# Cluster attention and two wide layers on one core: GpSimd in written order, the steps of a pair spread anew over its ticks, values' high halves on GpSimd

## The chip, the core and the metric

One core of a Trainium2 chip: TensorE (PE, matmuls; PEld its weight loads), VectorE (DVE), ScalarE (ACT), GpSimd (POOL), and SyncE (SP), whose queue issues this kernel's DMA transfers. The metric is the device time of one execution in microseconds (us).

## The reference

```python
def _attn_ref(q, k, v, centroids):
    ...
    q_assign = np.argmax(np.einsum('bhsd,hcd->bhsc', q_n, c_n), axis=-1)
    k_assign = np.argmax(np.einsum('bhsd,hcd->bhsc', k_n, c_n), axis=-1)
    mask = q_assign[:, :, :, None] == k_assign[:, :, None, :]
    scores = scale * np.matmul(q, k.transpose(0, 1, 3, 2))
    scores = np.where(mask, scores, -1000000000.0)
    scores = scores - np.max(scores, axis=-1, keepdims=True)
    attn = np.exp(scores)
    attn = attn / (np.sum(attn, axis=-1, keepdims=True) + 1e-09)
    return np.matmul(attn, v).astype(np.float32)

def _moe_ref(x, w_in, w_out, alpha):
    h = x @ w_in
    g = np.maximum(h, 0.0) + alpha * np.minimum(h, 0.0)
    return (g @ w_out).astype(np.float32)

def _moe2_ref(x, w_in, w_out):
    h = x @ w_in
    g = np.maximum(h, 0.0) + np.log1p(np.exp(-np.abs(h)))
    return (g @ w_out).astype(np.float32)
```

`q`, `k` and `v` are 2 x 8 heads x 768 x 64, with 16 centroids a head; `q_n`, `k_n`, `c_n` are the rows over their norms. A query attends only to keys of its own cluster. The heads side by side are the 1536 x 512 input of `_moe_ref` (2048 hidden units), whose output is that of `_moe2_ref`.

## The kernel before

*Numbers.* Products keep float32's precision with two fast matmul operands: a value is split into a rounded high half and the low rest (`hi`/`lo`, `ph`/`pl`, `xh`/`xl`, `gh`/`gl`, `vv` with both), and the products of the halves are summed in PSUM.

*Attention.* Heads go in 8 pairs (a batch and two heads). A pair has 12 units, one for each block of 128 queries of each head, and a loop of 96 **ticks** (lines 777 to 805) is a software pipeline over the units. In tick u, in this order, TensorE makes the scores of unit u (L586, L587: `ak`, `aq` are keys and queries, `mk`, `mq` carry the mask as 16 extra rows), ScalarE copies out a finished output (`drain`, every second tick), takes the exponentials of unit u-1 (L601), VectorE the maximum of unit u (L592); then the steps registered for the tick's early phase run; TensorE transposes unit u-2 (L614), ScalarE and VectorE split it into `ph` (L630) and `pl` (L634); TensorE multiplies with the values, `attend` (L644), for unit u-4; last run the steps of the late phase.

*Steps of a pair.* What has to be ready before pair n's units is cut into named steps (`steps_of`), and a table gives each its tick: value x means tick 12(n-2) + x, late phase; a half (6.5) means the next whole tick, early phase. The pair's own units are at x = 24 to 35. So each tick holds steps of pair n+2 (x under 12) and of pair n+1 (x from 12). `STEADY` serves most pairs, `FIRST`, `SECOND` and `THIRD` the first three; `PRELUDE` lists what comes before tick 0. The steps: `sq0/1` square the tokens, `fold0` to `fold2` sum them by halving, `inv0` to `inv2` make the inverse norm `rinv` (`inv_norm`, L127 to L141); `hik/hiq`, `lok`, `lq0/1` split keys and queries; `dk/dq` the centroid products (L397), `de` copies them out, `dt` transposes them, `dn` (L436) scales by `rinv`, `mx`, `eq`, `m2` find the best centroid, `ot` transposes the one-hot rows, `mr` makes the mask rows (L495 on ScalarE, L497 on VectorE); `op` copies operands by DMA (L536), `mk` the masks (L542, L543); `va` splits the values (L556, L557); `go` makes the pair ready. Loads are `load_tok`, `load_dim` and `load_v`, each with one buffer. `finish(n)` normalises a pair's output: at ticks +7 to +16 after the pair, with `rp`, a transposed reciprocal made by TensorE (L717) and multiplied in by VectorE (L721) at +12 and +14. `dps`, `dt`, `ot` and `rp` all use the one PSUM buffer with tag "m" (`ps_m`, bufs=1).

*Order.* Inside `tc.manual_schedule` the named engines, PE, ACT and DVE, execute in the order written; GpSimd and SP are ordered by the framework's scheduler, which works on its own timing model. Waits are generated from the tiles that are read and written. The manual part ends with the last unit (L781); the layers are ordered by the scheduler on all engines.

*Layers.* 16 blocks of hidden units each; weights arrive as 64-bit floats, are turned to float32 by ScalarE, VectorE and GpSimd (`to_float32`) and split. `first` makes hidden products (L843), `activate` and `complete` the activation (L855 to L884), `second` the output products (L902) into four accumulators, `close` adds them up (L917) and sends them out.

## Time and profile before

| | us |
|---|---|
| median of 3 runs (816.08 to 821.30) | 818.02 |
| the profiled execution | 819.76 |
| its span, first to last instruction | 817.8 |
| busy in the span: PE / DVE / ACT / POOL | 784.9 / 599.4 / 490.6 / 345.0 |
| mean granted TensorE clock | 0.976 |

The profile is of one execution. A row of the view of stretches has the stretch, its length, then busy us and, in brackets, instructions of PE, PEld, DVE, ACT and POOL, the granted clock, the DMA share and GB/s. Busy time of PE counts matmuls to a modelled end, so overlapping ones make it look fuller than it is. A row of a timeline has start, duration, engine, line, operation, written tile <- read tiles, shape, count, and in brackets the idle time of the engine before it and what ended that.

### The profile page before, as it was taken

Reading aid. Unit: us, or ns where it says so; the run is one execution under the profiler, and the core shown is the slowest. Engines: PE = TensorE matmul, PEld = TensorE weight load, DVE = VectorE, ACT = ScalarE, POOL = GpSimd, SP = SyncE. Lnnn points to the kernel's source line nnn. Section 1 sums busy time; section 2 is a strip of 40 time slices with the busy share of each in tenths; the row PEclk is TensorE's granted clock in tenths of the full one; section 3 lists DMA queues with packets and bytes.
Section 4 is the critical chain, followed back from the end, with each engine's and each line's share of the span. In section 5 each row is a group of like instructions: output and inputs, shape, how many; then the busy total and the mean of one; then the engine's idle time right before and its main releaser. Section 6 shows DMA issues by size and latency. Waiting matters only on the chain.

```text
span 817.8 us, 11947 instructions
## 1 busy us (share of the span) xinstructions
PE 784.9 (96%) x4137; PEld 672.7 (82%) x4137; DVE 599.4 (73%) x953; ACT 490.6 (60%) x992; POOL 345.0 (42%) x355
## 2 busy tenths in 40 slices
PE   7799999989999978999999999999999999999997
PEld 5699988989998767888888888888888888888886
DVE  5799989989999979446835934979459568764443
ACT  5589988978899868535635634675366245343221
POOL 3765766657244565215404503766045036023000
PEclk9599999999999998999999999999999999999999
DMA  9976675664451244201401401322013012000102
GB/s 256 235 178 152 167 181 134 158 163 103 100 160 42 79 147 161 79 1 60 148 0 52 135 20 52 97 85 77 1 52 130 25 52 77 27 1 1 43 35 77
DMA packets 27195, 76.50 MB, mean 94 GB/s; under 512 B 4512, under 2 KB 7456, under 8 KB 27136
## 3 DMA queue, kind: packets, MB, share of 16 engines
q1 hardware_dynamic: 27136, 75.75, 32.6%
q8 instruction: 32, 0.52, 0.3%
q14 instruction: 27, 0.22, 0.1%
HBM read 49.36 MB, written 3.15 MB: 64 GB/s over the span
## 4 chain that ended last, share of the span: by engine, by line
PE 76%; DVE 11%; DMA 5%; POOL 3%; issue 2%; ACT 2%; SPq 0%; DVEq 0%; POOLq 0%; ACTq 0%
PE acc L902 29%; PE hp L843 27%; PE pt L614 6%; PE o L644 6%; PE s L587 3%; PE s L586 3%; DVE r L173 2%; DVE pl L634 2%; DMA tok<-in_qk_tok_dram 2%; DVE nm L592 1%; DMA mq<-hi 1%; POOL t L178 1%; DVE m L168 1%; DMA mq<-mrow 1%; PE dps L397 1%
## 5 line engine op out<-in xcount | busy, mean ns | idle before, releaser
L843 PE MATMUL hp<-xh,ih 128*128 128x512 f32 x384 | 149.8, 391 | 2.7 <-DVE gl L884 2.4
L843 PE MATMUL hp<-xl,ih 128*128 128x512 f32 x384 | 150.0, 391 | 0.0
L843 PE MATMUL hp<-xh,il 128*128 128x512 f32 x384 | 149.7, 390 | 0.0
L181 POOL TENSOR_TENSOR il<-t,ih 128x512 fp32r<-128x512 f32 x32 | 43.9, 1372 | 197.5 <-ACT ih L180 187.1
L884 DVE TENSOR_TENSOR gl<-hp,gh 128x512 fp32r<-128x512 f32 x96 | 65.9, 687 | 70.8 <-ACT gh L883 70.6
L883 ACT CAST gh<-hp 128x512 fp32r<-128x512 f32 x96 | 56.5, 588 | 88.9 <-PE acc L902 69.0
L592 DVE TENSOR_REDUCE nm<-s 128x1 f32<-128x768 f32 x96 | 91.0, 948 | 11.9 <-PE s L587 11.4
L634 DVE TENSOR_TENSOR pl<-pt,ph 128x384 fp32r<-128x384 f32 x192 | 97.4, 547 | 1.9 <-ACT ph L630 1.2
L178 POOL TENSOR_TENSOR t<-m,r 128x512 uint32<-128x512 uint32 x64 | 85.2, 1331 | 29.3 <-DVE r L173 16.4
L601 ACT ACTIVATE e<-s,nm 128x768 f32<-128x768 f32 x96 | 87.9, 916 | 8.1 <-DVE nm L592 8.1
L614 PE MATMUL pt<-ident,e 128*128 128x128 f32 x576 | 85.4, 282 | 6.8 <-DVE pl L634 6.8
L630 ACT CAST ph<-pt 128x384 fp32r<-128x384 f32 x192 | 83.7, 490 | 13.6 <-PE pt L614 12.5
L843 PEld LDWEIGHTS hp<-xh,ih 128*128 128x128 f32 x384 | 72.2, 188 | 18.2 <-DVE gl L884 2.9
L865 ACT ACTIVATE sp<-a 128x512 f32<-128x512 f32 x48 | 30.4, 633 | 92.4 <-DVE a L861 92.4
L843 PEld LDWEIGHTS hp<-xh,il 128*128 128x128 f32 x384 | 72.4, 189 | 15.2
L843 PEld LDWEIGHTS hp<-xl,ih 128*128 128x128 f32 x384 | 72.2, 188 | 14.9
L614 PEld LDWEIGHTS pt<-ident,e 128*128 128x128 f32 x576 | 68.9, 145 | 17.2 <-DVE pl L634 12.6
L902 PE MATMUL acc<-gh,oh 128*128 128x512 f32 x192 | 73.8, 396 | 4.4 <-ACT gh L883 4.4
L902 PE MATMUL acc<-gl,oh 128*128 128x512 f32 x192 | 75.9, 396 | 0.2 <-DVE gl L884 0.2
L902 PE MATMUL acc<-gh,ol 128*128 128x512 f32 x192 | 75.5, 393 | 0.0
L586 PE MATMUL s<-ak,aq 128*128 128x384 f32 x192 | 70.6, 367 | 4.7 <-DMA mk<-lo 4.7
L902 PE MATMUL acc<-oh,gh 128*128 128x512 f32 x192 | 74.7, 389 | 0.0
(168 smaller groups left out, 1679.9 us busy)
## 6 DMA issues: line engine op xcount, KB each, us to landing
raw<-in_w_in_dram SPq DMA_DIRECT2D x32, 512.0 KB, 3.3
raw<-in_w_out_dram SPq DMA_DIRECT2D x32, 512.0 KB, 3.3
tok<-in_qk_tok_dram SPq DMA_DIRECT2D x8, 768.0 KB, 5.4
ak<-hi SPq DMA_DIRECT2D x32, 192.0 KB, 3.0
dim<-in_qk_dim_dram SPq DMA_DIRECT2D x6, 768.0 KB, 6.9
rawv<-in_v_dram SPq DMA_DIRECT2D x8, 384.0 KB, 3.2
aq<-hi SPq DMA_DIRECT2D x16, 192.0 KB, 3.7
mk<-lo SPq DMA_DIRECT2D x16, 192.0 KB, 3.4
```

The lines of the kernel that those rows point to most:

```text
L178: nc.gpsimd.tensor_tensor(out=t.bitcast(U32), in0=mu, in1=r, op=ALU.add)
L586: nc.tensor.matmul(s[:, c, 0:HS], lhsT=aq[:, qs], rhs=ak[:, ks], start=True, stop=False)
L592: nc.vector.tensor_reduce(out=nm, in_=st[u]["s"][:, :, 0:HS], axis=AX.XY, op=ALU.max, negate=True)
L601: nc.scalar.activation(out=e.rearrange("p (a j) c -> p a (j c)", a=2), in_=st[u]["s"][:, :, 0:HS], func=AF.Exp, bias=st[u]["nm"], scale=1. ...
L614: nc.tensor.transpose(pt[:, j * P : (j + 1) * P], st[u]["e"][:, 3 * a + j, :], ident)
L630: nc.scalar.copy(out=dh, in_=src)
L634: nc.vector.tensor_tensor(out=dl, in0=src, in1=dh.bitcast(F32), op=ALU.subtract)
L644: nc.tensor.matmul(acc[key][:, 0:QG], lhsT=vv[:, j, 2 * hh : 2 * hh + 2, :].rearrange("p a d -> p (a d)"), rhs=grp[key][part][:, j, :], st ...
L843: nc.tensor.matmul(hp, lhsT=a_[:, cs], rhs=b_[:, c, ts], start=n == 0, stop=n == 3 * NC_ - 1)
L883: nc.scalar.copy(out=gh, in_=hp)
L884: nc.vector.tensor_tensor(out=gl, in0=hp, in1=gh.bitcast(F32), op=ALU.subtract)
L902: nc.tensor.matmul(accs[c], lhsT=a_, rhs=b_, start=opens and n == 0, stop=closes and n == 2)
```

## The change

GpSimd joins the engines of the manual part. The loads become steps of their own (`lt`, `ld`, `lv`, and "values" in the prelude) in place of calls within `sq1`, `lq1` and `va`; SP stays with the scheduler. The operand copies and the values' split are cut into smaller steps (`op0a` to `op1c`, `va0`, `va1`). The values' high halves are copied by GpSimd, mask rows are all made on ScalarE, and the norm's scaling runs on the engine of its neighbours (GpSimd for all pairs but the first). The sum of a drained output is written one tick later, with a third buffer for `tmp` and `rest`. All tables are new, pair 1's squares and folds leave the prelude, and the last pair has a table of its own. In the last three steps of the last layer TensorE follows the written order.

```diff
 STEADY = dict(
-    hik=-1, lok=3, sq0=0, hiq=2, sq1=2, fold0=3, fold1=4, fold2=6, lq0=5, dk0=4, dq0=6, de0=6.5,
-    inv0=7, lq1=8, inv1=9, dk1=9, dq1=10, inv2=10, de1=10.5, dt=11, dn=11, op0=11, mx=11.5, eq=15,
-    m2=16, va=18, ot0=19, mr0=19, op1=19, ot1=20.5, mr1=20.5, mk0=20.5, mk1=20.5, go=22,
+    sq0=0, sq1=1, lt=1.5, fold0=2, hik=3, lok=3, hiq=4, lq0=5, dk0=5, fold1=6, dq0=6, de0=6.5, lq1=6,
+    fold2=7, ld=7, inv0=8.5, dk1=9, inv1=9, dq1=10, inv2=10, de1=10.5, dt=11, dn=12, mx=13, op0a=13.5,
+    op0b=14.5, op0c=15.5, eq=15.5, m2=17, ot0=19, mr0=19.5, ot1=20, va0=20, mr1=20.5, mk0=20.5, op1a=21,
+    op1b=22, va1=22, op1c=23, lv=23.5, mk1=24, go=23,
 )
 FIRST = dict(
-    mr0=23.5, mr1=23.5, mk1=23.5, va=24,
+    va0=24, mr0=25, mr1=25, mk1=25, op1c=25, va1=28, lv=29,
 )
 SECOND = dict(
-    dl0=12, dl1=12, inv0=12, de0=12.5, de1=12.5, inv1=13, inv2=13, dt=13, dn=14, mx=14, op0=14,
-    eq=15.5, m2=16, va=18, ot0=19, mr0=19, op1=19, ot1=20.5, mr1=20.5, mk0=20.5, mk1=20.5, go=22,
+    sq0=12.5, sq1=13, fold0=13, dl0=12, dl1=12, de0=12.5, de1=12.5, dt=13, lt=13, fold1=14, op0a=14,
+    fold2=15, op0b=15, inv0=15.5, op0c=16, inv1=16, inv2=16.5, dn=17, mx=17, eq=17.5, m2=18, ot0=19.5,
+    mr0=19.5, ot1=20, mr1=20.5, mk0=20.5, op1a=21, op1b=22, op1c=23, go=23, mk1=24, va0=25, va1=27, lv=28,
 )
 THIRD = dict(
-    hik=3, lok=3, sq0=0, hiq=4, sq1=2, fold0=4, fold1=5, fold2=6, lq0=5, dk0=5, dq0=6, de0=6.5,
-    inv0=7, lq1=8, inv1=9, dk1=9, dq1=10, inv2=10, de1=10.5, dt=11, dn=11, op0=11, mx=11.5, eq=15,
-    m2=16, va=18, ot0=19, mr0=19, op1=19, ot1=20.5, mr1=20.5, mk0=20.5, mk1=20.5, go=22,
+    sq0=5, sq1=7, lt=7.5, hik=7, lok=8, hiq=8, fold0=9, lq0=9, dk0=9, fold1=10, dq0=10, lq1=10, ld=10.5,
+    de0=10.5, dk1=11, fold2=11, inv0=11.5, dq1=12, inv1=12, de1=12.5, inv2=12.5, dt=13, dn=13.5, mx=14,
+    op0a=14.5, op0b=15.5, op0c=16.5, eq=16, m2=17, ot0=19, mr0=19.5, ot1=20, va0=20, mr1=20.5, mk0=20.5,
+    op1a=21, op1b=22, va1=22, op1c=23, lv=23.5, mk1=24, go=23,
 )
+LAST = dict(STEADY, op1a=19, op1b=20, va1=21, op1c=21, mk1=22, go=22)
 PRELUDE = [
     "warm 18", "sq0 0", "centroids_high", "red0 0", "centroids_low", "hik 0", "sq1 0", "lok 0",
     "red1 0", "hiq 0", "lq0 0", "dk0 0", "dq0 0", "inv0 0", "lq1 0", "inv1 0", "de0 0", "dk1 0",
-    "dq1 0", "inv2 0", "op0 0", "de1 0", "dt 0", "hik 1", "lok 1", "hiq 1", "warm 10", "dh0 1",
-    "dh1 1", "op1 0", "warm 10", "minus_alpha", "dn 0", "mx 0", "eq 0", "m2 0", "sq0 1", "sq1 1",
-    "fold0 1", "fold1 1", "fold2 1", "ot0 0", "lq0 1", "ot1 0", "rq0 0", "rk0 0", "rk1 0", "rq1 0",
-    "lq1 1", "go 0",
+    "dq1 0", "inv2 0", "op0a 0", "op0b 0", "op0c 0", "lt 0", "values", "de1 0", "dt 0", "hik 1", "lok 1",
+    "hiq 1", "warm 10", "dh0 1", "dh1 1", "op1a 0", "op1b 0", "warm 10", "minus_alpha", "dn 0", "mx 0",
+    "eq 0", "m2 0", "ot0 0", "lq0 1", "ot1 0", "rq0 0", "rk0 0", "rk1 0", "rq1 0", "lq1 1", "ld 1", "go 0",
...
-        nc.vector.tensor_scalar(out=s1, in0=s1, scalar1=0.5, scalar2=1e-6, op0=ALU.mult, op1=ALU.add)
+        eng.tensor_scalar(out=s1, in0=s1, scalar1=0.5, scalar2=1e-6, op0=ALU.mult, op1=ALU.add)
...
-            tc.manual_schedule(engines={mybir.EngineType.PE, mybir.EngineType.Activation, mybir.EngineType.DVE})
+            tc.manual_schedule(
+                engines={mybir.EngineType.PE, mybir.EngineType.Activation, mybir.EngineType.DVE, mybir.EngineType.Pool}
+            )
...
-        load_v(0)
...
-                if t == 1:
-                    load_tok(n + 1)
...
-                if t == 1 and n > 0:
-                    load_dim(n + 1)
...
-            def rows(t, eng):
+            def rows(t):
...
-                if eng is nc.scalar:
-                    nc.scalar.activation(out=q["mrow"][:, t, :], in_=src, func=AF.Identity, scale=mscale, bias=bias)
-                else:
-                    nc.vector.tensor_scalar(
-                        out=q["mrow"][:, t, :], in0=src, scalar1=mscale, scalar2=bias, op0=ALU.mult, op1=ALU.add
-                    )
+                nc.scalar.activation(out=q["mrow"][:, t, :], in_=src, func=AF.Identity, scale=mscale, bias=bias)
...
-            def operands(hh):
+            def operands(hh, part):
...
+                if part == 0:
+                    aq = ap3.tile([P, S], F32R, tag="aq", name="aq")
+                    ak = ap3.tile([P, S], F32R, tag="ak", name="ak")
+                    mq = ap3.tile([D + C, S], F32R, tag="mq", name="mq")
+                    mk = ap3.tile([D + C, S], F32R, tag="mk", name="mk")
+                    res.append((aq, ak, mq, mk))
+                aq, ak, mq, mk = res[hh]
...
-                ):
+                )[2 * part : 2 * part + 2]:
                     nc.sync.dma_start(out=dst.bitcast(F32), in_=src)
...
+                for part in range(3):
+                    st_[f"op{hh}" + "abc"[part]] = lambda hh=hh, part=part: operands(hh, part)
...
-            @step("va")
-            def _():
-                raw = vs.pop(n)
-                vv = ap2.tile([P, J, 4, D], F32R, tag="vv", name="vv")
-                for hh in range(2):
-                    s_hi, s_lo = (0, 1) if hh == 0 else (3, 2)
-                    nc.vector.tensor_copy(out=vv[:, :, s_hi, :], in_=raw[:, hh])
-                    nc.gpsimd.tensor_tensor(
-                        out=vv[:, :, s_lo, :], in0=raw[:, hh], in1=vv.bitcast(F32)[:, :, s_hi, :], op=ALU.subtract
-                    )
-                load_v(n + 1)
-                q["vv"] = vv
+            def values(hh):
+                if hh == 0:
+                    q["vv"] = ap2.tile([P, J, 4, D], F32R, tag="vv", name="vv")
+                    q["raw"] = vs.pop(n)
+                vv, raw = q["vv"], q["raw"]
+                s_hi, s_lo = (0, 1) if hh == 0 else (3, 2)
+                nc.gpsimd.tensor_copy(out=vv[:, :, s_hi, :], in_=raw[:, hh])
+                nc.gpsimd.tensor_tensor(
+                    out=vv[:, :, s_lo, :], in0=raw[:, hh], in1=vv.bitcast(F32)[:, :, s_hi, :], op=ALU.subtract
+                )
+
+            for hh in range(2):
+                st_[f"va{hh}"] = lambda hh=hh: values(hh)
+
+            st_["lt"] = lambda: load_tok(n + 1)
+            st_["lv"] = lambda: load_v(n + 1)
+            st_["ld"] = lambda: load_dim(n + 1)
...
-        def drain(key):
+        def drain(key, u):
...
-            tmp = ap4.tile([P, QG], F32, tag="tmp", name="tmp", bufs=2)
+            tmp = ap4.tile([P, QG], F32, tag="tmp", name="tmp", bufs=3)
...
-                rest = ap4.tile([P, QG], F32, tag="rest", name="rest", bufs=2)
+                rest = ap4.tile([P, QG], F32, tag="rest", name="rest", bufs=3)
                 nc.sync.dma_start(out=rest[main], in_=tmp[other])
-                nc.gpsimd.tensor_tensor(out=xs[main, cols], in0=rest[main], in1=tmp[main], op=ALU.add)
+                at(u + 1)(
+                    lambda: nc.gpsimd.tensor_tensor(out=xs[main, cols], in0=rest[main], in1=tmp[main], op=ALU.add)
+                )
...
+        plans = [FIRST, SECOND, THIRD] + [STEADY] * (len(pairs) - 4) + [LAST]
         for n in range(len(pairs)):
-            for name, x in ((FIRST, SECOND, THIRD)[n] if n < 3 else STEADY).items():
+            for name, x in plans[n].items():
                 todo[(n - 2) * UPP + int(-(-x // 1)), L if x % 1 == 0 else E].append(steps[n][name])
...
+            elif name == "values":
+                load_v(0)
...
     for k in range(NS):
+        if k == NS - 3:
+
+            ctx.enter_context(tc.manual_schedule(engines={mybir.EngineType.PE}))
         complete(k + 1)
```

## Rows read from the trace of the kernel before

**Rows 1.** The page, its first line

```profile
span 817.8 us, 11947 instructions
```

**Rows 2.** Stretches (pairs 0, 1, 2 to 5, 6): length, busy us, clock, DMA

```profile
23.44:59.41 35.97, 32.37 (x195) 29.50 (x194) 29.54 (x51) 26.40 (x62) 24.11 (x31) 0.76 0.83 205
59.41:88.44 29.03, 28.67 (x215) 26.71 (x214) 27.56 (x51) 26.31 (x62) 17.68 (x24) 1.00 0.69 170
88.44:215.54 127.10, 120.56 (x890) 113.72 (x889) 117.74 (x209) 109.12 (x257) 83.29 (x100) 0.97 0.59 143
215.54:242.01 26.47, 26.47 (x206) 25.34 (x205) 25.93 (x46) 23.92 (x57) 11.40 (x14) 1.00 0.50 109
```

**Rows 3.** Chain that ended last, 60 to 100: start, us, what

```profile
69.53 0.53 PE dps L397 x3
```

**Rows 4.** Groups by line, pairs 1 to 5: count, busy us, mean ns, idle

```profile
L556 DVE CAST vv<-rawv 128x384 fp32r<-128x384 f32 x10 | 6.3, 668 | 0.0
L139 DVE TENSOR_SCALAR s<-s 128x24 f32<-128x24 f32 x5 | 2.4, 473 | 0.0
L497 DVE TENSOR_SCALAR mrow<-ot,mscale,mbias 64x384 fp32r<-64x384 f32 x5 | 3.3, 658 | 0.0
L436 DVE TENSOR_TENSOR dn<-dt,rinv 128x384 f32<-128x384 f32 x6 | 3.3, 556 | 0.0
L476 POOL TENSOR_SCALAR oh<-dn 128x384 fp32r<-128x384 f32 x5 | 6.2, 1247 | 0.4
```

**Rows 5.** Timeline, 53.9 to 57.1 and 136.2 to 141.8, VectorE and GpSimd

```profile
54.02 2.90 POOL L326 TENSOR_TENSOR sq<-tok 128x768 f32<-128x768 f32 x2
...
55.48 1.47 DVE L139 TENSOR_SCALAR s<-s 128x24 f32<-128x24 f32 x1
...
137.21 2.12 DVE L556 CAST vv<-rawv 128x384 fp32r<-128x384 f32 x2
```

**Rows 6.** Timeline, 172 to 184, queue of SP and TensorE

```profile
173.19 0.33 SPq L232 DMA_DIRECT2D dim<-in_qk_dim_dram  x1
...
182.55 0.45 PE L587 MATMUL s<-mk,mq 80*128 80x384 f32 x1 [2.47 <-DMA mk<-mrow]
```

**Rows 7.** DMA issues from 172 to 176: count, KB each, median us to landing

```profile
dim<-in_qk_dim_dram SPq DMA_DIRECT2D x1, 768.0 KB, 9.0
mk<-mrow SPq DMA_DIRECT2D x2, 48.0 KB, 7.8
```

**Rows 8.** DMA issues from 236 to 239

```profile
mk<-mrow SPq DMA_DIRECT2D x2, 48.0 KB, 2.1
```

**Rows 9.** Timeline, 26 to 60, GpSimd and VectorE

```profile
29.80 1.47 POOL L326 TENSOR_TENSOR sq<-tok 128x768 f32<-128x768 f32 x1 [2.25 <-DMA tok<-in_qk_tok_dram]
...
31.50 1.42 DVE L139 TENSOR_SCALAR s<-s 128x24 f32<-128x24 f32 x1 [4.33 <-POOL s L137]
```

**Rows 10.** Timeline, 0 to 36

```profile
9.17 0.53 SPq L238 DMA_DIRECT2D tok<-in_qk_tok_dram  x1
...
18.17 1.57 ACT L324 ACTIVATE sq<-tok 128x768 f32<-128x768 f32 x2 [4.33 <-DMA tok<-in_qk_tok_dram]
...
20.47 1.26 DVE L510 TENSOR_SCALAR mk<-ot,mscale,mbias 16x384 fp32r<-16x384 f32 x2 [3.61 <-ACT mq L506]
...
21.79 0.66 PE L586 MATMUL s<-ak,aq 128*128 128x384 f32 x1 [4.73 <-DMA mk<-lo]
```

**Rows 11.** Timeline, 215 to 219, first tick of pair 6

```profile
216.41 0.55 DVE L448 TENSOR_REDUCE mx<-dn 128x24 f32<-128x384 f32 x1
...
216.70 0.49 PE L717 MATMUL rp__3353<-ident,rx 128*128 128x128 f32 x3
...
216.87 1.01 DVE L634 TENSOR_TENSOR pl<-pt,ph 128x384 fp32r<-128x384 f32 x2
```

**Rows 12.** Timeline, 808 to the end, VectorE

```profile
812.06 2.48 DVE L917 TENSOR_TENSOR y<-y,acc 128x512 f32<-128x512 f32 x4 [3.67 <-PE acc L902]
```

**Rows 13.** Timeline, 308 to 312, TensorE

```profile
308.99 2.07 PE L902 MATMUL acc<-gh,oh 128*128 128x512 f32 x4 [4.43 <-ACT gh L883]
```

More of the change, by code (lines that the diff above doesn't have):

```diff
@@ L516, in steps_of @@
                 st_[f"ot{t}"] = lambda t=t: onehot(t)
-                st_[f"mr{t}"] = lambda t=t: rows(t, nc.scalar if first_ or t == 1 else nc.vector)
+                st_[f"mr{t}"] = lambda t=t: rows(t)
                 st_[f"rq{t}"] = lambda t=t: straight(t, 0)
                 st_[f"rk{t}"] = lambda t=t: straight(t, 1)
-            def operands(hh):
+            def operands(hh, part):
                 rows = slice(hh * D, (hh + 1) * D)
                 hif, lof = q["hif"], q["lof"]
-                aq = ap3.tile([P, S], F32R, tag="aq", name="aq")
-                ak = ap3.tile([P, S], F32R, tag="ak", name="ak")
-                mq = ap3.tile([D + C, S], F32R, tag="mq", name="mq")
-                mk = ap3.tile([D + C, S], F32R, tag="mk", name="mk")
+                if part == 0:
[5 more added lines that the diff above has]
+                aq, ak, mq, mk = res[hh]
                 for dst, src in (
@@ L534, in operands @@
                     (aq[D:P], lof[rows, 0]),
-                ):
+                )[2 * part : 2 * part + 2]:
                     nc.sync.dma_start(out=dst.bitcast(F32), in_=src)
-                res.append((aq, ak, mq, mk))
             def masks(hh):
@@ L545, in steps_of @@
             for hh in range(2):
-                st_[f"op{hh}"] = lambda hh=hh: operands(hh)
+                for part in range(3):
+                    st_[f"op{hh}" + "abc"[part]] = lambda hh=hh, part=part: operands(hh, part)
                 st_[f"mk{hh}"] = lambda hh=hh: masks(hh)
-            @step("va")
-            def _():
-                raw = vs.pop(n)
-                vv = ap2.tile([P, J, 4, D], F32R, tag="vv", name="vv")
-                for hh in range(2):
-                    s_hi, s_lo = (0, 1) if hh == 0 else (3, 2)
-                    nc.vector.tensor_copy(out=vv[:, :, s_hi, :], in_=raw[:, hh])
-                    nc.gpsimd.tensor_tensor(
-                        out=vv[:, :, s_lo, :], in0=raw[:, hh], in1=vv.bitcast(F32)[:, :, s_hi, :], op=ALU.subtract
-                    )
-                load_v(n + 1)
-                q["vv"] = vv
+            def values(hh):
[13 more added lines that the diff above has]
+            st_["ld"] = lambda: load_dim(n + 1)
             @step("go")
@@ L784 @@
             if drains:
-                drain(drains.pop())
+                drain(drains.pop(), u)
             if 1 <= u <= NU:
```

## Prediction

> **What bounds the kernel now.** The page gives a span of 817.8 us [rows 1]; the profiled execution took 819.76, so 1.96 us lie outside the span and are kept as they are. Then I read the attention pair by pair with the view of busy time by stretches. The 96 ticks, in each of which TensorE takes one unit of scores, transposes and attention, start at 23.44, twelve to a pair of some 2.4 us; the larger part of the span follows them, in matmul-bound layers that the diff hardly touches. The stretches [rows 2] show pair 0 at 35.97 us, pair 1 at 29.03, pairs 2 to 5 at 127.10 together (31.8 each) and pair 6 at 26.47. In pair 6 TensorE is busy for 26.47 of 26.47: that is its floor with no wait. Pairs 1 to 5 also hold four rounds of centroid products, 0.53 us each in the chain [rows 3], so their floor is 26.47 + 4 x 0.53 = 28.6. Pairs 2 to 5 stand 127.1 - 4 x 28.6 = 12.7 us above it, pair 0 over 7. That is all that a better order in this stage can give; the rest of the kernel is matmuls.
>
> Then the timeline where ticks are long. Three causes stand out.
>
> *The shared port.* VectorE's 24-element scaling (L139) took 1.47 us from 55.48, ending at 56.95 where GpSimd's squares ended at 56.92; the two casts of the values (L556) took 2.12 us from 137.21 under GpSimd work [rows 5], against a mean of 0.67 each [rows 4].
>
> *The masks' transfers.* The load of the next pair's transposed inputs went out at 173.19, just ahead of the masks, and TensorE waited 2.47 us at 182.55 for a mask [rows 6]. In the DMA view the load took 9.0 us and the mk masks behind it 7.8 [rows 7]; with no such load ahead they land in 2.1 [rows 8].
>
> *GpSimd's order at the start.* The scheduler put pair 2's squares, which wait for a load, ahead of pair 1's norm; VectorE sat 4.33 us at L139 and then 1.42 in it, from 27.17 to 32.92 [rows 9].
>
> **The change part by part.**
>
> *VectorE is relieved.* Per pair it loses two casts (2 x 0.668), one scaling (0.473) and one mask row (0.658) [rows 4]: 2.47 us. It was busy for 117.74 of 127.10 in pairs 2 to 5 [rows 2], 29.4 a pair, about TensorE's floor; it falls to 27.0, so it stops being a joint bound. The longest single losses of this kind, the 2.12 us casts, go.
>
> *GpSimd takes two copies of 128x384 and a small scaling.* No copy of this form is in the trace. From below it is bounded by VectorE's 0.67, from above by GpSimd's own one-input operation of that size, 1.25 (L476) [rows 4]; I take 1.25, the same engine. GpSimd goes from 83.29/4 = 20.8 us a pair [rows 2] to 20.8 + 2 x 1.25 + 0.3 = 23.6 of some 30, not the bound (22.5 by the lower end). The new table spreads it: no tick holds more than the sq1, maximum-subtraction and xs trio. The trace shows the port conflict of [rows 5] directly. The Trainium skill, Perfetto Trace Analysis, section Optimizing Scalar/DVE Operations, says that GpSimd and VectorE share a read port, so that moving work between the two might not help. By that rule the relief would come back as waits of VectorE's remaining SBUF operations, and the time would be that of the second rival; here the trace agrees on the conflict, while most of VectorE's remaining work reads PSUM.
>
> *ScalarE takes the mask row*, about the 0.66 that VectorE had; it was busy 109.12/4 = 27.3 a pair [rows 2], so 27.9: under 28.6, close enough that I charge 0.4 us a pair for ticks in which it is late (tick 4 now has hiq, xh and a drain copy); without that cover the row costs its 0.66.
>
> *Dim load two ticks earlier.* lq1 moves from tick 8 to 6, and the load can go when lq1 has read the tile: about 5 us ahead of the masks instead of 0.4. With its 9.0 us [rows 7] the masks (still tick 20.5) then land at most some 4.5 us after issue, with 3 ticks of over 6 us to spare. The stall of [rows 6] goes; if I am wrong here, 2.5 us a time in two of the pairs stay.
>
> *A new wait: dn one tick later.* dn moves from 11 to 12, the tick in which finish() lets TensorE transpose the reciprocals into rp. Both dt and rp are the single PSUM buffer of tag m, so rp must wait until dn has read dt. Now rp starts at 216.70, straight after the attention matmuls, while VectorE's lows end at 216.87 + 1.01 = 217.88 [rows 11]. After the change dn (0.556, [rows 4]) follows those lows and rp follows dn. The maximum's 0.55 [rows 11] leaves that tick, so rp can start at 217.88 - 0.55 + 0.56 = 217.9 and TensorE stands about 1.2 us, with the next scores queued behind. From both sides: 0 if later ticks catch up wholly, 1.7 if VectorE is as late as now. TensorE is at its floor, so I take 1.25. It happens where rp of pair n-3 meets dn of pair n: in pairs 2 to 6, five times.
>
> Pairs 2 to 5: 28.6 + 1.25 + 0.4 = 30.25, times 4 = 121.0, against 127.1: -6.1. Pair 6: +1.25. Pair 1: nothing. Together **-4.9**.
>
> *Pair 0.* Pair 1's squares and folds leave the prelude for ticks 1 to 3, its norm goes to tick 4, pair 2's squares to tick 5 and after, and the written order keeps them so. The 5.75 us of [rows 9] go, and the 1.47 of [rows 5], 7.2 in all; ScalarE gets two squares in tick 1 and GpSimd is busy from the start. Between 4 and 7, I take **-5.5**.
>
> *The prelude.* First scores start at 21.79 after 4.73 us idle [rows 10]. Two things end there: the operands' transfers, queued behind pair 1's token load (issued 9.17), and the mask rows, which ended at 20.47 + 1.26 = 21.73 because ScalarE had stood 4.33 us for that load at 18.17 [rows 10]. The second cause goes with the squares. The first goes only if the load is issued behind the operands: the diff writes it there, but SP's order is the scheduler's, and it is ready first. Between 0 and 2.9 us (four mask rows of 0.66 in turn from about 17); I take **-1.5**.
>
> *The end.* The scheduler let all four accumulators close in the last four matmuls, so four additions of 2.48 us in all follow from 812.06 [rows 12]. In written order three of them run under the last matmuls: at most 1.86; since the last matmul ends a little after 812.06, **-1.2**, between 0 and 1.9.
>
> *Between the stages* nothing moves on paper, but the scheduler orders the layers anew; TensorE waits 4.43 us at 308.99 [rows 13], and this could be more or less: 0, with some 4 us to either side.
>
> Sum: 819.8 - 4.9 - 5.5 - 1.5 - 1.2 = 806.7. The median of the runs shown is 818.02, 1.7 lower than the profiled execution and within the spread of those three; I forecast **807**, and 1% of this kernel (8.2 us) is about what a measurement can tell from no change.
>
> **The rivals.**
>
> *No new wait.* rp's wait is caught up (0 in place of 1.25, five times: -6.2) and the operands overtake the token load (another -1.4): 799. For it: ticks after a stall run down to TensorE's pace. Against: that engine has no slack in pair 6 [rows 2].
>
> *GpSimd's order holds VectorE.* In tick 10 the last step of the norm stands behind the second values' copy and subtraction, and VectorE's reciprocal waits for it; its SBUF operations wait for the port more often. About 2 us in each of pairs 1 to 6: +12, so 819, no change. It decides if GpSimd comes to tick 10 over a microsecond late. For it: 23.6 of 30 us leaves little; against: reciprocal and dn are two ticks apart.
>
> *The drains hold GpSimd (slower).* xs waits in order for the rest transfer, which at tick 8 now goes out behind the dim load. Should that take its 9.0 us [rows 7], xs stands some 4 us past its tick, and the norm, rinv and dn behind it; VectorE, in order too, stops and TensorE with it. At 4 to 5 us in pairs 1 to 5: +20 to 25, so about 830. It decides if rest lands later than two ticks after its issue. Against: the load has a head start of a tick, and the pace of such loads varies.
>
> That the loads' new ticks change nothing, since SP's queue is the scheduler's, is in the bounds of the prelude.
>
> **How the numbers follow.** Forecast 0.55, its own range 801 to 813 by the bounds above; no new wait 0.22; GpSimd's order 0.15; the drains 0.08. Below 809.8 lie the second case and nearly three quarters of the forecast: faster by over 1% 0.62. Within 1%: the rest of the forecast and most of the third, 0.29. Slower 0.09. The range that leaves out under 2 in 10 reaches from 797 into the third case, 818.
>
> **What would show it.** Right: pair 0 near 30 us; no wait of TensorE for a mask; L139 gone from VectorE; rp in the ticks 24, 36, 48, 60 and 72 waiting about 1.2 us on dn; additions of y spread over the last 6 us. Wrong: waits of VectorE's reciprocal (L140) on GpSimd, or of xs on rest longer than now; first scores still at 21.8; TensorE idle for longer between the stages.

## The result, and the profile after

The changed kernel takes 822.55 us (median of 18 runs), the kernel before 816.25 us (18 runs beside them): a ratio of 1.0063, interval 1.0046 to 1.0081. It is 6.3 us slower where 807 was forecast, and lies above the forecast's range. In a second set of runs (c1, below) it was 823.13 us, ratio 1.0131 (1.0094 to 1.0168). Runs of the kernel before lie between 808.5 and 822.6 us within that set, those of the changed kernel between 819.9 and 825.6; so each ratio below is to runs of the kernel before that were made beside it. A ratio can differ by 0.2% from the quotient of the two medians, so a difference of 1 or 2 us between kernels that did not run side by side is open.

The two profiled executions hide the loss: the changed kernel's took 819.38 us, its fastest run, and that of the kernel before 819.76. A second profile of the kernel before (c2) is of an execution of 813.16 us; the median of 816.25 lies about midway between its two. First the changed kernel in the view of stretches (pair 0, pair 1, pairs 2 to 5, pair 6; columns as in [rows 2]), with its span:

```profile
span 817.3 us, 11944 instructions
22.78:55.69 32.91, 28.77 (x183) 25.41 (x182) 25.83 (x40) 27.43 (x62) 20.85 (x26) 0.88 0.73 182
55.69:87.16 31.47, 30.57 (x227) 27.78 (x226) 26.59 (x49) 27.28 (x66) 25.76 (x35) 1.00 0.70 185
87.16:215.88 128.72, 117.93 (x890) 111.16 (x889) 112.72 (x194) 111.90 (x261) 89.29 (x112) 1.00 0.58 142
215.88:243.76 27.88, 26.78 (x206) 25.38 (x205) 25.38 (x45) 24.74 (x60) 12.39 (x16) 1.00 0.52 119
```

The same stretches in the second profile of the kernel before (span 811.2 us):

```profile
23.35:60.71 37.36, 31.25 (x192) 28.29 (x191) 29.74 (x51) 26.33 (x60) 22.82 (x30) 0.84 0.76 195
60.71:90.26 29.55, 28.90 (x218) 27.02 (x217) 27.58 (x51) 26.43 (x63) 19.22 (x24) 1.00 0.69 167
90.26:208.78 118.52, 117.19 (x890) 110.73 (x889) 115.92 (x208) 109.23 (x257) 83.84 (x100) 1.00 0.63 153
208.78:235.28 26.50, 26.50 (x206) 25.38 (x205) 25.91 (x46) 23.93 (x57) 11.41 (x14) 1.00 0.50 109
```

From these rows and [rows 1, 2], in us, the changed kernel's first profile against each of the two of before:

| stretch | forecast | against the first profile | against the second |
|---|---|---|---|
| up to the first tick | -1.5 | 22.78 - 23.44 = -0.7 | -0.6 |
| pair 0 | -5.5 | 32.91 - 35.97 = -3.1 | -4.4 |
| pair 1 | 0 | 31.47 - 29.03 = +2.4 | +1.9 |
| pairs 2 to 5 | -6.1 | 128.72 - 127.10 = +1.6 | 128.72 - 118.52 = +10.2 |
| pair 6 | +1.25 | 27.88 - 26.47 = +1.4 | +1.4 |
| pair 7, the layers, the end | -1.2 | 573.5 - 575.8 = -2.3 | -2.4 |
| sum | -13.1 | -0.5 | +6.1 |

Against the second profile the loss sits in pairs 2 to 5, and the last two columns say why the forecast saw room there: the 127.1 us of [rows 2] are not what the kernel takes each time. In the second profile these pairs take 28.98, 29.34, 29.49 and 30.72 us; TensorE waits for no mask within them (0.65 us just ahead of them, 1.22 at the end of pair 0), and once, 1.19 us, behind the casts. Of the 8.6 us between the two profiles 3.4 are TensorE's own busy time (120.56 against 117.19): the mean granted clock was 0.97 in the first and 1.00 in the second, and in the first it was 0.95 in pairs 3 and 5, those that follow the two waits for masks, and 1.00 in pairs 2 and 4. The rest are waits. Pairs 2 to 5 of the first profile, one by one:

```profile
88.44:119.29 30.85, 29.15 (x224) 27.73 (x223) 28.42 (x52) 26.82 (x65) 21.71 (x26) 1.00 0.67 162
119.29:151.50 32.21, 31.03 (x224) 29.29 (x223) 30.46 (x53) 27.88 (x65) 21.08 (x26) 0.95 0.59 151
151.50:183.39 31.89, 29.42 (x224) 27.61 (x223) 28.73 (x53) 26.67 (x65) 21.51 (x26) 1.00 0.64 157
183.39:215.54 32.15, 30.95 (x224) 29.09 (x223) 30.14 (x53) 27.74 (x66) 18.99 (x25) 0.95 0.47 105
```

In the changed kernel, by contrast, pairs 2 to 5 are alike to 0.02 us (32.17 to 32.19), so what holds them is in the order itself. The waits of TensorE in these four pairs, whole:

```profile
PE pt L617 <- DVE pl L637: 6.3, 4, 1.6
PE rp__1834 L722 <- DVE dn L436: 1.1, 1, 1.1
PE rp__2842 L722 <- DVE dn L436: 1.1, 1, 1.1
PE rp__2338 L722 <- DVE dn L436: 1.1, 1, 1.1
PE rp__1330 L722 <- DVE dn L436: 1.1, 1, 1.1
```

The lower four are the forecast's new wait, at the place and nearly the size that it gave (1.25). The upper one, 1.6 us in each pair's fifth tick, it did not have. It is read from three engines in the timeline of one pair: VectorE's eq (L459), GpSimd, and TensorE behind both:

```profile
130.50 2.23 DVE L459 SCALAR_TENSOR_TENSOR dn<-dn,rank 128x384 f32<-128x384 f32 x1
132.65 0.55 DVE L637 TENSOR_TENSOR pl<-pt,ph 128x384 fp32r<-128x384 f32 x1
...
125.52 0.84 POOL L450 TENSOR_TENSOR dn<-dn,mx 128x384 f32<-128x384 f32 x1 [5.99 <-DVE mx L448]
126.32 1.47 POOL L330 TENSOR_TENSOR sq<-tok 128x768 f32<-128x768 f32 x1
127.86 0.74 POOL L674 TENSOR_TENSOR xs<-rest,tmp 64x256 f32<-64x256 f32 x1
128.68 1.84 POOL L347 TENSOR_TENSOR sq<-sq 128x768 f32<-128x768 f32 x1
130.48 1.83 POOL L373 TENSOR_TENSOR lo<-dim,hi 128x768 fp32r<-128x768 f32 x1
...
133.25 1.01 PE L617 MATMUL pt<-ident,e 128*128 128x128 f32 x6 [1.58 <-DVE pl L637]
```

eq takes 0.55 us where nothing meets it (the least in this trace), here 2.23: it starts 0.02 us behind GpSimd's split of the keys (lok, 1.83 us) and ends 0.42 after it. GpSimd is in lok at that moment because it stood 5.99 us for the late maximum (4.89 with dn back, e1) with four instructions behind it in written order.

### The profile page after: what moved, and what is told of

The parts are those of the page before. It is cut to its first block, busy times and chain, and to the rows that moved or that the text cites. A ratio compares the mean times of both kernels' runs of the same rounds, so it can differ in the third digit from the quotient of the medians.

```text
span 817.3 us, 11944 instructions
## 1 busy us (share of the span) xinstructions
PE 779.9 (95%) x4137; PEld 667.7 (82%) x4137; DVE 587.7 (72%) x923; ACT 493.7 (60%) x999; POOL 355.9 (44%) x378
## 4 chain that ended last, share of the span: by engine, by line
PE 73%; POOL 8%; DVE 7%; issue 6%; ACT 4%; DMA 2%; SPq 0%; POOLq 0%; ACTq 0%; DVEq 0%
PE acc L910 29%; PE hp L851 27%; PE pt L617 5%; PE o L647 5%; PE s L589 3%; PE s L590 3%; DVE r L176 2%; POOL sq L330 2%; POOL t L181 1%; POOL sq L347 1%; PE dps L397 1%; DMA aq<-lo 1%; DVE pl L637 1%; DVE y L925 1%; DVE m L171 1%
## 5 line engine op out<-in xcount | busy, mean ns | idle before, releaser
L181 POOL TENSOR_TENSOR t<-m,r 128x512 uint32<-128x512 uint32 x64 | 85.2, 1330 | 27.7 <-DVE r L176 13.4
L910 PE MATMUL acc<-ol,gh 128*128 128x512 f32 x192 | 74.7, 389 | 0.0
```

The costliest lines, as they stand in the source:

```text
L181: nc.gpsimd.tensor_tensor(out=t.bitcast(U32), in0=mu, in1=r, op=ALU.add)
L910: nc.tensor.matmul(accs[c], lhsT=a_, rhs=b_, start=opens and n == 0, stop=closes and n == 2)
```

## The experiments

The edits are to the tables of the changed kernel unless said otherwise; names are shortened in them. "Ticks" are the distances between starts of nm on VectorE.

**c1, the changed kernel again.** No edit.

> The changed kernel as it is, once more, beside the kernel before and the three edits on the same chip. If the changed kernel's loss is steady, it stands 0.3 to 0.9% above the kernel before (some 819 to 824 us), and its pairs 2 to 5 take 32.2 us each again, with TensorE idle 1.1 us at the reciprocals' transposes and 1.6 us in the fifth tick of each pair. If the loss lay in the order of the layers rather than in the attention, the part behind the last tick would be longer than the 544.8 us of the first profile.

823.13 us, ratio 1.0131. Three of pairs 2 to 5 took 32.17 to 32.20 us again, one, pair 2, 33.75; waits of 1.10 to 1.14 and 1.57 to 1.60 us at the same places. In pair 2 the granted clock was 0.66 from 103 to 108 us, right behind the wait of 1.60. From the last scores to the last matmul it took 542.96 us against 540.99 in the first profile: one and the same program, so 2 us there are no effect of an edit. The part behind the last tick's start took 546.0 us, where the kernel before has 547.2 and 547.3, so the loss is not there. Pair 0 took 34.10, against 32.91.

**e1, dn back.**

```
-    ... dt=11, dn=12, mx=13, ...
+    ... dt=11, dn=11, mx=13, ...
```

> Only dn goes back from tick 12 to tick 11 (pairs 3 to 7). Theory (the wait of rp for dn is on the path): the first tick of pairs 2 to 6 falls from 3.76 to about 2.65 us, TensorE's idle 1.1 us there goes, five times, and the time falls by about 5.5 us against the changed kernel (to about 817). Rival (VectorE sets the pace in these ticks anyway, so the wait only comes back in the next ticks): pairs 2 to 6 stay within 0.4 us of 32.2 and 27.9 and the time within 2 us of the changed kernel.

811.64 us, ratio 0.9969 (0.9944 to 0.9994): 11.5 us under c1, twice what was expected, and a little faster than the kernel before. The rival falls. Both waits went, not one. Pairs 2 to 5 hold no idle time of TensorE, 119.90 busy of 119.90:

```profile
89.33:209.23 119.90, 119.90 (x892) 110.03 (x889) 105.30 (x194) 110.73 (x261) 89.58 (x111) 1.00 0.62 152
```

The fifth tick fell from 3.9 to 2.36 us, though nothing there was edited. VectorE and GpSimd at the same place as above:

```profile
128.77 0.63 DVE L459 SCALAR_TENSOR_TENSOR dn<-dn,rank 128x384 f32<-128x384 f32 x1
...
128.94 2.15 POOL L373 TENSOR_TENSOR lo<-dim,hi 128x768 fp32r<-128x768 f32 x1
```

eq now starts 0.17 us ahead of lok, takes 0.63, and it is lok that takes longer, 2.15 instead of 1.83. So the late dn costs twice: 1.1 us where rp waits for it, and, since the three ticks behind it are no shorter in the changed kernel than in e1, and so do not catch that up, eq then comes to its place just after lok instead of just before, 1.6 us more. Not all of this is won: the sixth tick is longer in e1 (4.03 us against 2.72), and pairs 2 to 6 are 10.5 us shorter together.

**e2, norm first.**

```
-    ... va1=22, op1c=23, lv=23.5, ...
+    ... va1=23, op1c=23, lv=24, ...
```

> Only the second half of the values goes one tick later (va1 22 to 23, its next load lv 23.5 to 24; 21 to 22 in the last pair), so GpSimd does the last step of the norm before it. Theory (GpSimd's order holds VectorE at the reciprocal): VectorE's wait of 1.3 us before the second reciprocal goes, the eleventh tick of pairs 1 to 5 falls from 3.38 to 2.3 us or less, and the time falls by 1 us per pair, about 5 us. Rival (TensorE has work queued in that tick and is not idle, as the trace shows no gap of it there): the tick is shorter and the next one longer by the same, the pairs stay at 32.2 within 0.3 us and the time within 1.5 us of the changed kernel.

821.96 us, 1.2 under c1 (ratio 1.0108, interval 1.0072 to 1.0144). The wait that the forecast's rival named is there in the changed kernel and gone in e2:

```profile
149.54 0.30 DVE L143 RECIPROCAL rinv<-s 128x24 f32<-128x24 f32 x1 [1.32 <-POOL s L142]
```

In e2 the reciprocal follows pl at 147.66 without a wait. The eleventh tick falls from 3.38 to 2.35 and the next rises from 1.76 to 2.79; pairs 2 to 5 stay at 32.17 to 32.21. GpSimd's order does hold VectorE 1.3 us a pair, and it costs nothing, since TensorE has work queued: the expectation's rival holds.

**e3, eq clear of lok.**

```
+EARLY = dict(sq1=0, fold0=0, hik=2, lok=2)
-  ... + [STEADY] * (len(pairs) - 4) + [LAST]
+  ... + [STEADY] + [dict(STEADY, **EARLY)] * (len(pairs) - 5) + [dict(LAST, **EARLY)]
```

> In the tables of pairs 4 to 7 alone, GpSimd's second squares and first fold go to tick 0 and the split of the keys (hik, lok) to tick 2, so that GpSimd is not in lok when VectorE does eq. Theory (eq waits for the port while GpSimd's 1.83 us lok runs): eq takes 0.6 us instead of 2.2, the fifth tick of pairs 2 to 5 falls from 3.92 to about 2.4 us, TensorE's 1.6 us idle there goes, four times, and the time falls by about 6 us against the changed kernel. Rival (ScalarE is the late one in that tick, with hiq and xh there beside the copies and the exponential): eq is short but the tick stays above 3.4 us, the time within 2 us of the changed kernel. A third way: the squares and the fold, now in tick 0, meet dn or mx instead and the same 1.6 us is lost there.

815.87 us, 7.3 under c1 (ratio 1.0030, interval 1.0001 to 1.0060). No eq of pairs 3 to 6 takes over 0.8 us; TensorE's idle 1.6 us is gone from pairs 2 to 5, which take 30.81 to 30.84 us; the 1.1 us for dn stays. The sixth tick, in which TensorE has more to do, rises from 2.72 to 3.70, so 1.35 of 1.6 us a pair is kept.

**e4, the three edits together.**

> The three edits of the first experiments together: dn back at tick 11, the second half of the values one tick later, and in pairs 4 to 7 the squares, the fold and the split of the keys earlier. With dn alone, pairs 2 to 5 took 29.97 us with no idle of TensorE in the trace. Theory (TensorE is the bound there, and the forecast's floor of 28.6 us was too low): pairs 2 to 5 stay at 29.5 to 30.2 us and the time within 2 us of dn alone. Rival (VectorE's remaining waits, eq for the port and the reciprocal for GpSimd, still set the pace, although TensorE shows no gap): pairs 2 to 5 fall to about 28.6 us, and the time is some 5 us below dn alone.

809.77 us, ratio 0.9922 (0.9892 to 0.9952). Pairs 2 to 5:

```profile
89.48:207.43 117.95, 117.72 (x890) 110.45 (x889) 107.23 (x193) 109.92 (x260) 89.40 (x112) 1.00 0.63 155
```

29.5 us a pair: 0.5 below e1, not the 1.4 of the rival. The gains of e1 and e3 don't add: in the profiles pairs 2 to 6 are 10.5 and 5.4 us shorter alone, 12.1 together, as they would be where e1 already removes both waits. (The times, 13.4 us under c1 by medians and 17.1 by ratios, come from two sets of runs and can't tell.) And this best order of the steady pairs, 117.95, is hardly under the 118.52 of the kernel before in its second profile.

**e5, the kernel before with dn late alone.**

```
-    ... dn=11, op0=11, mx=11.5, ...      (the kernel before)
+    ... dn=12, op0=11, mx=13, ...
```

> The kernel before with one step of the change alone: dn at tick 12 and the maximum behind it at 13, as the change has them, GpSimd's order the scheduler's as before. Theory (dn in that tick costs the wait of rp by itself): TensorE waits 1.1 to 1.3 us for dn at the first reciprocals' transpose of pairs 2 to 6, and the time rises by 5 to 7 us over the kernel before. Second theory (most of the price came by the knock-on in the fifth tick, where eq ran into GpSimd's lok in the written order): 5 to 7 us here against 11 us in the changed kernel. Rival (the late dn only hurts because GpSimd waits in written order behind the late maximum): under 3 us here.

822.54 us, ratio 1.0071 (1.0042 to 1.0100), 6.0 us over the kernel before. TensorE stands 1.17 us at the first reciprocals in four of the five pairs and 0.44 in the fifth, for example

```profile
98.06 0.52 PE L717 MATMUL rp__1344<-ident,rx 128*128 128x128 f32 x3 [1.17 <-DVE dn L436]
```

The wait alone is worth about what the forecast gave it (five times 1.25; the interval allows 3.4 to 8.2 us). In this profile too the fifth tick of pairs 2 to 6 takes 2.25 to 2.29 us. Without the written order of GpSimd the knock-on stays out: the second theory holds.

**e6, GpSimd out of the written order.**

```
-  engines={PE, Activation, DVE, Pool}
+  engines={PE, Activation, DVE}
```

> The changed kernel with GpSimd taken out of the written order again, so the scheduler orders GpSimd and only the tables, the copies and the rest of the change stay. Theory (the written order lets eq meet lok in the fifth tick; another order would avoid it in most pairs, but may put squares that wait for a load ahead of a norm): the 1.6 us idle of the fifth tick goes in most pairs, pair 0 and 1 are longer by up to 3 us, and the time is 2 to 6 us under the changed kernel. Rival (the written order is worth what the change wants of it): the time is 3 us or more above the changed kernel, with VectorE waiting for GpSimd at the norm.

848.99 us, ratio 1.0408 (1.0376 to 1.0440): 26 us over c1 (not run beside it), and far past either figure expected. In pair 0 the scheduler put copies of the values, which waited 4.95 us for a load, ahead of most of pair 1's folds; TensorE stood 7.06 us there. In pairs 2 to 5 the waits are

```profile
PE ot L486 <- POOL oh L476: 6.6, 4, 2.3
PE pt L617 <- DVE pl L637: 5.0, 11, 1.1
```

beside the four for dn. So with these tables GpSimd's written order is what makes them work at all; the fifth tick's wait is a small price within it.

**e7, copies of the values on VectorE.** On top of e1.

```
-  nc.gpsimd.tensor_copy(out=vv[:, :, s_hi, :], in_=raw[:, hh])
+  nc.vector.tensor_copy(out=vv[:, :, s_hi, :], in_=raw[:, hh])
```

> The changed kernel with dn back at tick 11, and besides that the two copies of the values' high halves on VectorE again. Theory (VectorE has slack, since TensorE shows no idle with dn back): pairs 2 to 5 rise from 29.97 us by under 0.5 us each, and the time by 0 to 2 us over dn alone. Rival (the copies on VectorE fall under GpSimd's instructions and wait for the port, as the 2.12 us of the kernel before): each pair gains a wait of TensorE of about 1.2 us, and the time is 5 us or more above dn alone.

815.26 us, ratio 0.9994 (0.9972 to 1.0017): 2.0 us over e1 by the ratios, 3.6 by the medians of two sets of runs. Pairs 2 to 5 take 30.35 to 30.44, 0.4 each over e1, with the copies unhindered at 0.35 us; in pair 1 both a copy and an eq met GpSimd:

```profile
69.26 1.85 DVE L554 CAST vv<-rawv 128x384 fp32r<-128x384 f32 x1
...
72.82 1.55 DVE L459 SCALAR_TENSOR_TENSOR dn<-dn,rank 128x384 f32<-128x384 f32 x1
```

and that pair is 1.7 us longer. The theory holds for the steady pairs, the rival for one place. The offload is worth some 2 to 4 us.

**e8, the kernel before with the early load alone.**

```
-    inv0=7, lq1=8, ...       (the kernel before)
+    inv0=7, lq1=6, ...
```

> The kernel before with one step of the change alone: the second half of the scaled queries' low part (lq1) at tick 6 instead of 8, so the next pair's transposed inputs can be loaded about two ticks earlier, away from the masks. Theory (the load right ahead of the masks costs the 1.7 and 2.5 us that TensorE waited for masks in two pairs): no wait of TensorE for a mask in pairs 1 to 6, and the time falls by 2 to 6 us. Rival (the load meets the operands' or the rest transfers instead, or the waits are caught up in the next ticks): within 1.5 us of the kernel before.

815.90 us, ratio 0.9982 (0.9950 to 1.0014). TensorE waits for no mask in pairs 2 to 6 (1.48 us once, in pair 0's last tick), but casts met GpSimd in two pairs (1.67 and 1.64 us, after casts of 1.87 and 1.86). The time is that of the kernel before, as the rival has it, though the interval leaves room for a gain of up to 4 us. The waits of [rows 6] are not in every execution of the kernel before, as c2 shows from the other side.

**c2, the kernel before again.**

> The kernel before once more, with a second profile of it. If the profiled execution on which the forecast was summed (819.76 us) was one with more than its usual stalls, this one has another time within 808 to 823 us, and the difference lies in pairs 0 to 5, in waits for transfers (a mask, an operand, the token loads), while its ticks without a wait agree with the first profile.

813.16 us; its stretches stand in the section on the result. Agreed in pairs 2 to 5, 118.52 us in place of 127.10, with part of that the clock and not waits; pairs 0 and 1 were 1.4 and 0.5 us longer.

**e9, pair 2's squares behind eq; e10, transfers in written order; c3, e11, e12.** All on top of e4.

```
e9, e11:       -    sq0=5, sq1=7, ...   (pair 2)
               +    sq0=6, sq1=7, ...
e10, c3, e11, e12:
               -  engines={PE, Activation, DVE, Pool}
               +  engines={PE, Activation, DVE, Pool, SP}
e12:           the first mask row of pairs 1 to 7 by nc.vector.tensor_scalar, as before
```

> The kernel with the three edits, and in pair 2's table the first squares at tick 6 instead of 5, so that in pair 0 GpSimd does them after the one-hot steps and is idle when VectorE does eq. Theory (in pair 0, as in the steady pairs, eq waits for the port): eq of pair 0 takes 0.6 instead of 1.8 us, TensorE's 2.3 us idle there falls to 1.0 or less, pair 0 goes from 34.1 to about 33 us, and the time falls by 1 to 1.5 us. Rival (GpSimd is busy without a break for the rest of pair 0, and its work moved back meets the two steps of the scaled queries' low part instead): pair 0 and 1 together stay at 65.9 us within 0.7.

**e9.** 808.06 us, ratio 0.9886 (0.9844 to 0.9928), 1.7 under e4 by medians (not run beside it). eq of pair 0 is free and TensorE's 2.31 us idle there falls to 1.06, but a later step then meets GpSimd for longer (1.77 us in e4):

```profile
48.74 2.13 DVE L382 SCALAR_TENSOR_TENSOR lo<-dim,hi 128x384 fp32r<-128x384 f32 x1
...
48.65 1.81 POOL L347 TENSOR_TENSOR sq<-sq 128x768 f32<-128x768 f32 x1
```

Pair 0 takes 32.70 us and pair 1 31.66, 1.5 less together than in e4; but the changed kernel, without the edit, has 32.91 or 34.10 in pair 0, so this alone tells nothing.

> The kernel with the three edits, and the queue of transfers (SP) put in written order too. Theory (in the prelude pair 1's token load goes out ahead of the operands' transfers only because the scheduler orders SP): the first operands' transfers go ahead of it, the first scores start 2 to 3 us earlier (18.5 to 19.5 us instead of 21.8), and the time falls by 2 to 3 us if nothing else changes. Rival (a transfer that is late in written order holds those behind it): TensorE waits for masks or operands in later pairs, and the time is 3 us or more above the kernel with the three edits.

**e10.** 805.27 us, ratio 0.9860 (0.9822 to 0.9899), 4.5 under e4 by medians, 5.1 by ratios. The queue of SP, in e10 and then in the changed kernel:

```profile
11.65 0.56 SPq L534 DMA_DIRECT2D aq<-lo  x1
12.27 0.89 SPq L243 DMA_DIRECT2D tok<-in_qk_tok_dram  x1
...
8.97 0.53 SPq L243 DMA_DIRECT2D tok<-in_qk_tok_dram  x1
9.60 0.80 SPq L534 DMA_DIRECT2D aq<-hi  x1
```

With the operands ahead of the load, TensorE's first scores start at 16.75 and wait then only for the mask; in the changed kernel they start at 21.12 (21.92 in e4):

```profile
18.19 0.44 PE L590 MATMUL s<-mk,mq 80*128 80x384 f32 x1 [1.05 <-DVE mk L505]
...
21.12 0.66 PE L589 MATMUL s<-ak,aq 128*128 128x384 f32 x1 [4.27 <-DMA aq<-lo]
```

The first tick starts at 19.34, in e4 at 23.58. The theory holds, above its figure; no wait of TensorE for a transfer took its place, though in pair 0 one for ScalarE's copy of the centroid products grew from 1.05 to 2.23 us.

> The kernel with the three edits and the transfers in written order once more, as the base of the two beside it: 804.3 to 806.9 us again, first scores near 18.2 us, pairs 2 to 5 at 29.5 us, pair 0 at 32.7 us.

**c3.** 806.45 us, ratio 0.9887 (0.9837 to 0.9937). Pair 0 took 34.08 us, though, and 32.69 in e10: the same program. The premise that written transfers fix pair 0 is wrong.

> The three edits, the transfers in written order, and pair 2's first squares at tick 6 instead of 5. With the transfers in one order the luck of the loads is the same in both, so this tells whether the edit itself shortens pair 0. Theory (eq waits for the port in pair 0): eq there takes 0.6 instead of 1.8 us, TensorE's idle of 2.31 us falls to 1.1 or less, pair 0 takes 31.4 us instead of 32.7, and the time falls by about 1.3 us against the base. Rival (GpSimd's work moved back holds a later step, the split of the keys or the queries' low part, as a tick of 4.65 us in the earlier run suggests): pair 0 stays within 0.4 us of 32.7 and the time within 0.6 us of the base.

**e11.** 804.28 us, ratio 0.9863 (0.9818 to 0.9908): 2.2 us under c3, which ran beside it, where the theory gave 1.3 and the rival 0.6 at most. Yet pair 0, at 33.57 us, is where neither has it. eq's wait goes as in e9 (the seventh tick 2.91 instead of 4.16, TensorE's idle 1.07), but ticks 7 to 10 of pair 0 sum to 12.64 us, against 12.47 in e10 and 14.13 in c3. What is won at eq is lost at the next step, or the execution's own spread covers it; the runs don't settle which, nor where the gain in time comes from (by ratios it lies within the intervals, and e10, the same program as c3, is at 805.27).

> The three edits, the transfers in written order, and the first of the two mask rows of pairs 1 to 7 back on VectorE. The forecast charged ScalarE 0.4 us a pair for this row. Theory (neither engine is late in that tick): pairs 2 to 5 stay at 29.5 within 0.1 us and the time within 0.6 us of the base. Rival (the charge was right, ScalarE is late): pairs 2 to 5 fall by 0.4 us each, the time by 2 us or more. Third way (VectorE is the late one now): pairs 2 to 5 rise by 0.3 us or more each.

**e12.** 807.72 us, ratio 0.9905 (0.9871 to 0.9940). Pairs 2 to 5 take 29.93 to 29.95 us, 0.45 each over c3: the third way. The row is better on ScalarE.

## Why the forecast was wrong, step by step

**Where the error lies.** For the profiled execution the sum forecast -13.1 us and -0.5 came, 12.6 apart. Half of it is eq's meeting with lok, 4 x 1.57 = 6.3 us, for which the sum had nothing (it comes of the step on dn, below). Pair 0 and pair 1 are 2.4 each, the prelude 0.8; the floor with ScalarE's charge, 29.0 forecast against 29.49 in e4, is 4 x 0.49 = 2.0. Against that, the wait for dn was 0.5 smaller over the four pairs and the rest of the kernel 1.1 better. Another 3.2 us of the distance to 822.55 are that this execution was the fastest of 18.

**The base (wrong for the saving, not for the time).** The step that sets pairs 2 to 5 at 12.7 us above their floor took one execution for the kernel. Of those 12.7 us, 8.6 are absent from the second profile (127.10 against 118.52), and e8 finds no measurable gain in taking the cause of the mask waits away. That the wait for a mask stood in two of four alike pairs was a sign of it. This is why the forecast expected a gain over the kernel before in these pairs; what they would take after the change, 4 x 30.25, was summed from the floor and does not rest on it.

**The floor of 28.6 (too low by 0.4 to 0.9).** It was pair 6 plus four rounds of centroid products; pair 6 lacks dt's transposes too, which the sum left out. The pairs with no or hardly any idle time of TensorE take 28.98 (the first of c2's four), 29.5 (e4) and 29.97 (e1) with the same matmuls, so a full TensorE does not show a floor: its busy time runs to modelled ends. e3, which keeps the wait for dn and is rid of the other, has 30.82 where 30.25 was forecast, so the term itself was near; the saving from it was not.

**dn one tick later (right in size, wrong in reach).** The wait was called at 1.25 in the first ticks of pairs 2 to 6; it measured 1.10 to 1.15 there, and e5 finds it alone to cost 6.0 us. The step that failed is the one that takes these five waits as the whole price, "with the next scores queued behind": it follows TensorE alone. Counted from the start of the pair, VectorE came to eq 1.7 us later than in e1 (130.50 - 119.33 against 128.77 - 119.31) and GpSimd to lok 1.5 later, so that the two changed places: 1.57 us more in four pairs, which e1 removes by moving dn and e3 by moving lok. Together they explain the 11.5 us between c1 and e1 (5 x 1.1 + 4 x 1.57 = 11.8), which is more than the whole loss.

**GpSimd's order holds VectorE (rival; the time near, one part right).** The place named, tick 10 behind the values' second half, has its wait of 1.32 us, but e2 shows it costs nothing. The other half of the rival, that "SBUF operations wait for the port more often", is what happened, at a place that it did not name: the fifth tick, under lok. The rival's 819 is nearer than the forecast's 807, but half of its reason was wrong. The Trainium skill, Perfetto Trace Analysis, section Optimizing Scalar/DVE Operations, which the forecast weighed, says only that the two share a read port, so that such moves might not help. The Trainium skill, SBUF — State Buffer, section Who interferes with whom, is sharper: a VectorE instruction with two inputs in SBUF contends with a GpSimd instruction that reads SBUF, the shared ports are an exclusive lock, and the order of issue decides who waits. The traces agree, with both orders: eq behind lok 2.23 us against 0.55, lok behind eq 2.15 against 1.83. The forecast had [rows 5] for it and looked for such pairs only among the moved instructions, not for an unmoved eq.

**VectorE is relieved (half right).** It fell from 29.4 to 112.72 / 4 = 28.2 us a pair where 27.0 was forecast; without eq's waits, four times 1.65 us, it would be 26.5 (e1: 105.30 / 4 = 26.3). The two copies are worth 0.4 us a pair (e7) and the mask row 0.45 (e12), where the forecast gave the row a charge of 0.4 with the other sign. GpSimd's copy was taken at 1.25 us, bounded by 0.67 from below; it measured 0.50, outside both bounds.

```profile
L554 POOL CAST vv<-rawv 128x384 fp32r<-128x384 f32 x8 | 4.0, 498 | 0.0
```

**Pair 0 and pair 1 (mechanism right, the gain mostly given back).** The 4.33 us of VectorE behind the squares [rows 9] are gone, and the mean clock in pair 0 is 0.88 of full against 0.76 in [rows 2] (0.84 in c2). Pair 0 gained 3.1 to 4.4 of 5.5 us in the first profile, 1.9 to 3.3 in c1. But eq waits there too (1.81 us, under the squares), and part of pair 2's steps went from pair 0 into pair 1: TensorE's matmuls went from 195 to 183 in pair 0 and from 215 to 227 in pair 1, whose busy time on TensorE rose from 28.67 to 30.57 us. Pair 1 lost 1.9 to 2.4 where "nothing" was written. The two pairs together gained 0.6 to 2.5 us in the first profile, and in c1 between 1.1 won and 0.8 lost. With these tables the written order was needed even for that: in e6 pair 0 takes 43.64 us.

**The prelude (wrong choice within its bounds).** 0.6 to 0.7 us of the 1.5 came in the first profile, in c1 0.1. The doubt in the text, that "SP's order is the scheduler's, and it is ready first", is what holds: the load left at 8.97, ahead of the operands. e10 shows that cause to be worth 4.2 us at the first tick (19.34 against 23.58 in e4), more than the upper bound of 2.9.

**The end (right).** From the end of the last matmul to the end of the last addition it took 1.84 us before and 0.73 after, -1.1 for -1.2. The four additions now start 2.0 us ahead of the last matmul's end, where those of [rows 12] started 0.6 ahead:

```profile
811.48 2.73 DVE L925 TENSOR_TENSOR y<-y,acc 128x512 f32<-128x512 f32 x4 [2.32 <-PE acc L910]
```

**Between the stages (0, with 4 to either side: right).** The waits that answer to [rows 13] are 5.45 us in one execution of the changed kernel and 4.45 in another, and 5.42 in c2.

**The drains hold GpSimd (rival, did not happen).** xs waited 1.6 us in all in pairs 2 to 5.

The best of these kernels, e11 at 804.28 and e10 at 805.27 us, beat the kernel before by 1.4% and the changed one by some 2%. Of the 18 us between the medians of c1 and e10, 11.5 go to dn (c1 and e1 ran side by side), some 2 to eq's clear place and the norm, and 4.5 to the order of the transfers; the last two compare separate sets of runs.

## What to carry to other kernels

When a step is moved later, follow the delay through every engine whose order is fixed, not only to the engine that waits, and look there for an instruction pair that shares a port and now swaps order: here a wait of 1.1 us brought one of 1.6 four ticks on. Before summing savings from a profile, ask of each stall whether every alike iteration has it; one that two of four pairs show may be gone in the next execution, and a second profile of the same kernel is the cheapest test. When a step moves from one stretch to the next, count its work there. Putting an engine in written order takes away what the scheduler did well along with what it did badly, so the tables have to be right to a fraction of a microsecond.

## What the runs showed of the hardware that was not expected

- GpSimd copied 128x384 from float32 in 0.50 us, less than half of its own one-input operation with a scalar on that size (1.17 us in the same stretch) and little over VectorE's unhindered 0.35 (e7).
- Two executions of one program differ in a whole stage by more than the edits do: 1.4 us in pair 0 (c3 and e10), 8.6 us in pairs 2 to 5 of the kernel before (3.4 of them TensorE's busy time at a lower clock), 2 us in the layers.
- In the prelude a transfer went out only when the eighth before it had landed: in e4 one left at 18.63 after a landing at 18.61, the next at 19.33 after 19.31, at 20.28 after 20.27 and at 21.05 after 21.03. The program's own waits set this: in the trace the transfers take turns with eight semaphores that they raise when they land, and each of these issues waits on the one it will raise. So the operands' transfer at 18.63 stood 2.4 us for the token load, of which it reads nothing.
